# Seeding of old sums, staging rows, operand splits and the first group's order in a fused attention + MLP kernel

## The chip, the cores and the metric

The kernel runs on one core of a Trainium2 chip. The metric is the time of one execution in microseconds of device time. The kernel before took a median of 1314.25 us over three runs (1311.72 to 1316.65).

A core has TensorE (PE: matmuls from SBUF into PSUM), VectorE (DVE), ScalarE (ACT), GpSimd (POOL) and SyncE (SP). Each works through its own queue in program order and waits on semaphores. DMAs are issued from the queues of SP and POOL; those that add to their destination ("accumulating" DMAs) are issued from POOL.

## What is computed

x is 2048 x 576, float32. The reference, cut to what matters:

```python
def A(x):                                   # wqkv 576 x 1728, wo 576 x 576
    q, k, v = heads(x @ wqkv)               # 32 heads of 18
    logits = q . k[s - 2*w], w = 0..7       # sliding window of 8, dilation 2
    return softmax(logits) @ v -> @ wo

def B(x):                                   # w1, w2 576 x 576, w3 576 x 4608, w4 4608 x 576
    x1 = x + shift4(gelu(layernorm(x) @ w1)) @ w2
    return x1 + gelu(layernorm(x1) @ w3) @ w4

xn = layernorm(x)
out = x + A(xn) + B(xn)
```

## The kernel before, in words

**Number format.** Operands of matmuls are split into a rounded high part and a low part, and a product is the sum of high·high, high·low and low·high. With 576 = 4.5 blocks of 128 rows this makes 14 matmuls for one contraction (PAIRS), 7 for one over half the channels (HALVES). A "split" is: ScalarE writes the high part, VectorE subtracts it from the raw value.

**Stages.** (1) QKV, 0 to 195 us: for each token block of 128, `q_cg` and `q_half` make column groups of 432 and 864 of x @ wqkv; `q_half` uses the two banks of a PSUM tile, 512 and 352 columns. (2) Mixing by w1 and w2, 195 to 313 us. (3) Phase 1 of the big MLP, 313 to 535 us: 16 windows u = 0 .. 15 (z = u - 16). A window makes two "up" tiles (`up`: 14 matmuls of 512 columns, then GELU by ScalarE to a high part and a full copy, and VectorE's low part) and four "down" tiles of the window before (`down`: 12 matmuls of 288 columns for a token block of 128, in both banks of a PSUM tile). (4) Phase 2, 535 to 1241 us: 28 groups q = 0 .. 27 of seven products (`product`, 7 matmuls each), named P1, P2, P6, P5, P7, P4, P3, in the manner of Strassen: sums of quarters of xn (A: B11, B21, B22, T1 to T4) against sums of weight blocks (`combine` makes them from w3 in place in the tile w3st; `split_a` and `split_s` split them to w3a and w3s). Results are added over products in Z1 to Z4 (`keep` copies by ScalarE, `z_add` adds by VectorE), then GELU (`gelu12`, `gelu22`: high part; `low12`, `low22`: low part), and eight down tiles D0 to D7 of the group before, in between the products. A group takes some 24 us. The first group has the four down tiles of the last window instead. (5) Output projection by wo, 1241 to 1312 us. The attention itself runs on VectorE in small steps behind the phases (`bg`), paced by a debt to which `spent` is charged.

**Where the sums live.** The 16 row blocks of the result are summed over windows and groups. For ten of them (YD = 1, 2, 3, 5, 7, 9, 10, 11, 13, 15) the sum is in DRAM (yd): ScalarE drains PSUM into a staging row (L870) and POOL issues an accumulating DMA from it to yd[t] (L871). In phase 1 from window 2 on and in phase 2 the staging rows are three rows of the tile Y, 9, 11 and 10 (`EV[0]`), used in turn: a drain waits until the DMA of three drains before has read its row. For the other six (t = 0, 4, 6, 8, 12, 14) the sum is in SBUF, in Y[:, t]: before the tile's matmuls ScalarE copies the old sum into PSUM ("seed", `ahead`, L846), the matmuls add to it, and ScalarE copies the whole back (L873).

**Order.** `ahead` makes the PSUM tile that is needed next as soon as a down tile has been drained: three tiles are in turn in phase 1, two in phase 2. So the seed of the tile after next, or the first matmul of an unseeded one, waits for the drain of the tile that had the bank. Everything is issued in program order, and where a split of an operand stands in the code it stands in ScalarE's queue. In phase 1 `get_op` loads the first operands B11, B21, T3, T2, T1 by SP, and `split_op` splits them in the last two windows. In phase 2 `plan` hangs such steps behind the items of a group's order string (`ORDER`, `ORDERS`).

**Other queues.** `load_xa(t)` adds x into yd[t] by an accumulating DMA of POOL (L880), once for each t of YD, in windows 4 to 13. `sums` makes the operand sums T1 to T4 in DRAM, by DMAs of SP and POOL (L900, L901). In each split of weights POOL issues a small accumulating DMA from w3st into w3a or w3s (L963), and `combine` (L955) can overwrite w3st only after it.

Of the kernel before, what the change touches and what calls it, by code (L numbers as in the profile page):

```python
# [57 lines left out]
def fused_block(ctx, tc, x, wqkv, wo, w1, w2, w3, w4, out):  # L58
# [259 lines left out]

    def q_half(t, h):
        ps = psb.tile([128, 2, 512], F32, name="ps", tag="b")  # L320
        xs, c = lhs(t), 2 * h * CG
        for i, (a, b) in enumerate(PAIRS):
            for k, (n0, n1) in enumerate(((0, 512), (512, 2 * CG))):
                pe.matmul(ps[:, k, :n1 - n0], xs(a), WQ[:, b, c + n0:c + n1],  # L324
                          start=i == 0, stop=i == len(PAIRS) - 1)
        stg = qpool.tile([128, 2 * CG], F32, name="stg", bufs=4)
        act.copy(stg, ps.rearrange("p i c -> p (i c)")[:, :2 * CG])  # L327
        if t == NT - 1 and h == 1:
            get(("z", 1), ring_block(("z", 1)))
        spill(stg, t, 2 * h * CG, 2 * CG)  # L330
# [506 lines left out]
    def halves(t):  # L837
        return Y[:, t, :].rearrange("p (h c) -> p h c", h=2)

    def ahead():  # L840
        n = bank["next"]
        if n < len(bank["order"]):
            t = bank["order"][n]
            ps = bank["make"](n)
            if t not in YD:
                act.copy(ps[:, :, :HF], halves(t))  # L846
            bank["open"].append((t, ps))
            bank["next"] = n + 1

    def begin_downs(order, bufs, make):  # L850
# [4 lines left out]

    def down(t, parts):
        col = slice(t % 4 * 128, (t % 4 + 1) * 128)
        due, ps = bank["open"].pop(0)
        assert due == t
        seq = []  # L860
        for h, w in parts:
            seq += [(h[:, 0], w, 0), (h[:, 0], w, 1), (h[:, 1], w, 0)]
        for n, (h, w, p) in enumerate(seq):
            for k in range(2):
                pe.matmul(ps[:, k, :HF], h[:, col], w[:, p, k * HF:(k + 1) * HF],  # L865
                          start=n == 0 and t in YD, stop=n == len(seq) - 1,
                          skip_group_check=True)
        if t in YD:
            e = staging()
            act.copy(e.rearrange("p (h c) -> p h c", h=2), ps[:, :, :HF])  # L870
            pool.dma_start(yd[t], e, accum_op=ALU.add)  # L871
        else:
            act.copy(halves(t), ps[:, :, :HF])  # L873
        ahead()

    xagain = {}
# [117 lines left out]
    XADD = {5: 0, 6: 4, 7: 8, 8: 12, 10: 6, 12: 14}  # L994
    for u, (c, b) in enumerate(units):
        if u == 1:
            begin_downs([4 * units[v][1] + j for v in range(NU - 1) for j in range(4)], 3,
                        lambda n: psb.tile([128, 2, 512], F32, name="ps", tag="b"))
        if u == 2:
            EV[0] = (9, 11, 10)  # L1000
            ntp.__exit__(None, None, None)
            ap_pool = apc.__enter__()
            state["gen"] = attention(ap_pool)
            next(state["gen"])
        z = u - NU
        if z == -2:
            rtemps[:] = [2, 13, 15]
        r = 0.0 if u < 4 else (RATE[0] if z < -2 else RATE[1]) / 6
        for i in range(C):
            bg(r - spent[0], False)  # L1010
            spent[0] = 0.0
            up(u, c, b, i)
            if u % 4 == 3 and i == 1 and c < NPL - 1:
                split_w3(2 * c + 3)
            if (u, i) == (0, 0):
                get_n(2, x1n[2])
                load_w3p(1, (0,))
            for t in LATE.get((u, i), ()):
                n_turn(t, ntpool)
            if (u, i) == (0, 1):  # L1020
                get_n(3, x1n[3])
            if (u, i) == (3, 0):
                pool.dma_start(yd[13], Y[:, 13, :])
                pool.dma_start(yd[15], Y[:, 15, :])
            if (u, i) in ((1, 0), (2, 1)):
                split_n(u + 1, x1n[u + 1], 0, RT)
            if z == -2:
                split_op(0, ("B11", "B21")[i])
            if z == -1:
                split_op(0, ("T2", "T1")[i])  # L1030
            if (z, i) == (-1, 1):
                x1 = ring_block(("w", 1))
                for sb in range(2):
                    area[sb].update(T4=x1[:, 0:5, :], B22=x1[:, 5:10, :])
                get_op(0, "B22")
                get_op(0, "T4")
        if u == 1:
            raw = x1n[3].bitcast(F32)
            pool.tensor_tensor(RS[2][:, 0, 0:1], raw[:, 4, 0:1], raw[:, 8, 0:1], op=ALU.mult)
        for j, (t, parts) in enumerate(prev):  # L1040
            bg(r - spent[0], j % 2 == 1)
            spent[0] = 0.0
            down(t, parts)
            if (u, j) == (2, 0):
                load_w3p(1, (1,))
                load_w4(1)
            if (u, j) == (3, 1):
                next(state["gen"])
            if u in (1, 2) and j == 1:
                split_n(u + 1, x1n[u + 1], 1, RT)  # L1050
            for f in {(-3, 1): (lambda: split_a(0),), (-3, 2): (lambda: split_w4(NPL),),
                      (-3, 3): (lambda: combine(0),),
                      (-2, 1): (lambda: split_op(0, "T3"),), 
                      (-1, 0): (lambda: split_s(0, (0, 1)),), (-1, 1): (lambda: split_s(0, (2,)),),
                      (-1, 2): (lambda: load_pair(1),)}.get((z, j), ()):
                f()
            if u % 4 == 2 and j == 1 and c < NPL - 1:
                split_w3(2 * c + 2)
# [18 lines left out]
        if z == -2:  # L1077
            x0 = ring_block(("w", 0))
            for sb in range(2):
                area[sb].update(T2=x0[:, 0:5, :], T1=x0[:, 5:10, :])  # L1080
            for k in ("T2", "T1"):
                get_op(0, k)
# [15 lines left out]
    begin_downs([4 * units[NU - 1][1] + j for j in range(4)]  # L1098
                + [8 * (g // NWP) + (j + 4) % 8 for g in range(2 * NWP) for j in range(8)], 2,
                lambda n: qpd.tile([128, 2, 512], F32, name=f"ps{n % 2}"))  # L1100
    Z1, Z2, Z3, Z4 = temp(13), temp(15), temp(5), temp(7)
    NQ = 2 * NWP
# [64 lines left out]
    def o_turn(t):  # L1167
# [275 lines left out]
```

## Time and profile before

| | us |
|---|---|
| median of three runs | 1314.25 |
| the profiled execution | 1313.82 |
| its span, first to last instruction | 1312.0 |
| TensorE busy | 1263.2 |
| VectorE busy | 905.5 |
| ScalarE busy | 766.1 |
| POOL busy | 259.1 |

The profile is of one execution. Busy times of engines overlap, so they don't add up to the span: the engine with the largest share, and what it waits for, tell what sets the time. The mean granted clock of TensorE over the span was 0.988 of full speed. In rows of the timeline the brackets give the idle time of the engine before the row and what ended it.

### The profile page before, as it was taken

What the parts mean: (1) busy time and instruction counts of PE and PEld (TensorE: products, weight loads), DVE (VectorE), ACT (ScalarE), POOL (GpSimd) and SP (SyncE); (2) the same over time, 40 slices, a digit from 0 to 9 for tenths busy, and PEclk for the clock granted to TensorE, in tenths of its full rate; (3) what the DMA queues carried; (4) which work ended last, traced back from release to release, by engine and by line L of the source; (5) the groups of instructions that cost most, each with busy time, mean ns of one, the idle gap of its engine ahead of it and who ended that gap; (6) DMA issues with size and microseconds to landing.
All of it is one profiled execution on the core that took longest, in us unless ns stands there. A gap on an engine that the chain in (4) does not pass through costs nothing.

```text
span 1312.0 us, 20032 instructions
## 1 busy us (share of the span) xinstructions
PE 1263.2 (96%) x7482; PEld 1148.2 (88%) x7482; DVE 905.5 (69%) x1194; ACT 766.1 (58%) x1220; POOL 259.1 (20%) x374
## 2 busy tenths in 40 slices
PE   8999999999999897789999999998999999999998
PEld 8988888899898786688898998987989999989898
DVE  6456535778368795449999999988999974446342
ACT  4322236436645545667677777768768767667730
POOL 2011100021123221112222222212222222222100
PEclk9999999999999898899999999999999999999999
DMA  7646874256788998568978777796776866899982
GB/s 212 153 107 151 171 156 144 71 162 178 175 257 199 197 202 224 103 156 143 223 172 179 185 157 141 174 248 159 149 164 140 172 126 126 200 213 218 254 251 82
DMA packets 204641, 226.14 MB, mean 172 GB/s; under 512 B 79856, under 2 KB 139728, under 8 KB 204416
## 3 DMA queue, kind: packets, MB, share of 16 engines
q1 hardware_dynamic: 171408, 157.60, 41.9%
q0 software_dynamic: 33136, 67.26, 31.8%
q8 instruction: 59, 0.97, 0.3%
q14 instruction: 38, 0.31, 0.1%
HBM read 125.76 MB, written 107.28 MB: 178 GB/s over the span
## 4 chain that ended last, share of the span: by engine, by line
PE 63%; DMA 14%; issue 8%; ACT 6%; DVE 5%; SPq 2%; POOL 2%; POOLq 0%; ACTq 0%; DVEq 0%
PE ps L865 20%; PE cc L1112 12%; PE ps L324 10%; PE p L830 6%; PE ps L214 6%; PE ps L470 4%; DMA w3st<-in_B_w_dram 3%; PE ps L313 3%; DMA w3a<-w3st 3%; DMA x1n<-xn 2%; POOL yd L871 1%; DMA Y<-in_B_w_dram 1%; DMA Y<-od 1%; DMA yd<-Y 1%; DVE w3st L955 1%
## 5 line engine op out<-in xcount | busy, mean ns | idle before, releaser
L865 PEld LDWEIGHTS ps<-w,c 128*128 128x128 f32 x3456 | 482.7, 190 | 50.6 <-ACT Y L870 23.5
L865 PE MATMUL ps<-w,c 128*128 128x288 f32 x3456 | 497.5, 297 | 29.7 <-ACT Y L870 21.4
L871 POOL DMA_DIRECT2D yd<-Y x154 | 138.9, 926 | 413.1 <-ACT Y L870 354.6
L824 DVE TENSOR_TENSOR c<-Y,c 128x512 fp32r<-128x512 f32 x144 | 98.8, 686 | 81.6 <-ACT Y L813 73.5
L1112 PE MATMUL cc<-xt,w3s 128*128 128x512 f32 (+1 forms) x588 | 149.3, 393 | 0.0
L870 ACT COPY Y<-ps 128x576 f32<-128x576 f32 x154 | 97.7, 636 | 74.7 <-PE ps L865 56.9
L324 PE MATMUL ps<-WQ,xt 128*128 128x512 f32 (+1 forms) x672 | 134.9, 360 | 0.0
L324 PEld LDWEIGHTS ps<-WQ,xt 128*128 128x128 f32 x672 | 116.7, 188 | 14.7
L1112 PEld LDWEIGHTS cc<-xt,w3s 128*128 128x128 f32 (+1 forms) x588 | 107.6, 188 | 21.1 <-DVE Y L1122 0.4
L1112 PE MATMUL cc<-x1n,w3a 128*128 128x512 f32 x392 | 100.1, 395 | 2.3 <-ACT cc L1304 2.3
L873 ACT COPY Y<-ps 128x576 f32<-128x576 f32 x108 | 68.9, 638 | 39.8 <-PE ps L865 38.4
L744 DVE TENSOR_TENSOR po<-q,k 128x2304 f32<-128x2304 f32 (+1 forms) x40 | 82.9, 2074 | 8.8 <-DMA k<-qkvd 6.3
L1112 PEld LDWEIGHTS cc<-x1n,w3a 128*128 128x128 f32 x392 | 70.7, 188 | 15.1 <-ACT cc L1304 2.7
L747 DVE TENSOR_REDUCE L<-po 128x128 f32<-128x2304 f32 (+1 forms) x40 | 82.8, 2070 | 0.6
L121 POOL TENSOR_TENSOR rs<-rs,mhalf 128x1 f32<-128x1 f32 x48 | 31.0, 645 | 258.8 <-DVE rs L120 147.8
L327 ACT COPY stg<-ps 128x864 f32<-128x864 f32 x24 | 21.2, 882 | 102.9 <-PE ps L324 60.2
L955 DVE TENSOR_TENSOR w3st<-w3st 128x384 f32<-128x384 f32 x108 | 60.2, 557 | 27.2 <-issue 16.1
L720 DVE TENSOR_TENSOR po<-v,L 128x1152 f32<-128x1152 f32 x56 | 75.4, 1354 | 1.0
L846 ACT COPY ps<-Y 128x576 f32<-128x576 f32 x108 | 69.6, 645 | 2.7
L724 DVE TENSOR_TENSOR po<-po 128x1152 f32<-128x1152 f32 x49 | 66.4, 1355 | 1.0
L1122 DVE TENSOR_TENSOR Y<-cc,Y 128x512 f32<-128x512 f32 x57 | 39.1, 685 | 32.7 <-ACT Y L1118 27.9
L1112 PE MATMUL cc<-x1n,w3s 128*128 128x512 f32 (+1 forms) x196 | 51.6, 404 | 8.7 <-ACT Y L1118 8.7
(193 smaller groups left out, 1889.7 us busy)
## 6 DMA issues: line engine op xcount, KB each, us to landing
yd<-Y POOLq DMA_DIRECT2D x156, 288.0 KB, 6.1
Y<-in_B_w_dram SPq DMA_DIRECT2D x31, 576.0 KB, 6.9
w3st<-in_B_w_dram SPq DMA_DIRECT2D x60, 256.0 KB, 6.4
qkvd<-stg SPq DMA_DIRECT2D x24, 432.0 KB, 3.5
yd<-ev POOLq DMA_DIRECT2D x26, 288.0 KB, 6.5
w3st<-in_B_w_dram SPq DMA_DIRECT2D x108, 64.0 KB, 6.4
xd<-st SPq DMA_DIRECT2D x16, 320.0 KB, 6.1
xd<-big SPq DMA_DIRECT2D x16, 320.0 KB, 8.2
```

The source lines that it names most:

```text
L214: pe.matmul(ps[:, h, :n], xs(a), ws(b, h), start=i == 0, stop=i == len(PAIRS) - 1)
L324: pe.matmul(ps[:, k, :n1 - n0], xs(a), WQ[:, b, c + n0:c + n1], start=i == 0, stop=i == len(PAIRS) - 1)
L720: dve.tensor_tensor(dst, vv, Lf[:, :, w:w + 1].to_broadcast([128, TPP * GH, HD]), op=ALU.mult)
L744: dve.tensor_tensor(dst, qf[:, None, :].to_broadcast([128, n, TPP * GC]), win, op=ALU.mult)
L747: dve.tensor_reduce(Lw[:, w:w + n, :], dst.rearrange("p w (x d) -> p w x d", d=HD), axis=AX.X, op=ALU.add)
L824: dve.tensor_tensor(h[:, 1, :], g, h[:, 0, :].bitcast(F32), op=ALU.subtract)
L830: pe.matmul(ps, W3[f][:, w, :], x1n[b][:, a, :], start=n == 0, stop=n == len(PAIRS) - 1)
L865: pe.matmul(ps[:, k, :HF], h[:, col], w[:, p, k * HF:(k + 1) * HF], start=n == 0 and t in YD, stop=n == len(seq) - 1, skip_group_check=True)
L870: act.copy(e.rearrange("p (h c) -> p h c", h=2), ps[:, :, :HF])
L871: pool.dma_start(yd[t], e, accum_op=ALU.add)
L955: dve.tensor_tensor(st[:, :, o, :], st[:, :, o, :], st[:, :, i, :], op=op)
L1112: pe.matmul(ps, WX[w][:k, v, SLOT[w], :], area[sb][xk][:k, a, :], start=onto is None and i == 0, stop=last and i == len(HALVES) - 1, skip_ ...
```

## The change

Six edits:

1. `q_half` makes its 864 columns as two halves of 432, one in each bank, and ScalarE copies the two halves to the same staging tile.
2. Seeding becomes a choice per tile. A tile that is not in YD is seeded in phase 1 only where its operands come from windows 3 to 11 (`down` runs one window later), and in phase 2 everywhere but for the four tiles of the last window and the tiles that groups 13 and 14 take over from groups 12 and 13 (g + 1 = 13 or 14). That makes 16 unseeded tiles: four with operands of windows 0 to 2, six with operands of windows 12 to 15, six in groups 13 and 14. Where it isn't seeded, the matmuls start at zero and VectorE adds PSUM to Y[:, t] (the new line L873 of the changed kernel).
3. The staging rows are five (9, 11, 10, 13, 15) from window 4 on, and three again from window 13 on (z = -3).
4. `load_xa` of the ten tiles in YD moves from windows 4 to 13 to groups 1 to 10 of phase 2, behind P3.
5. The loads of T2 and T1 are issued within window 14; the splits of the first operands move: B11 and B21 behind the third and fourth down tile of window 14, T3 and T2 behind the up tiles of window 15, T1 behind its fourth down tile.
6. The first group's order ends "D1 D2 P4 D3 P3" instead of "D1 D2 P3 P4 D3", and what hangs behind its items is placed anew.

```diff
 def q_half(t, h):
     ps = psb.tile([128, 2, 512], F32, name="ps", tag="b")
-    xs, c = lhs(t), 2 * h * CG
-    for i, (a, b) in enumerate(PAIRS):
-        for k, (n0, n1) in enumerate(((0, 512), (512, 2 * CG))):
-            pe.matmul(ps[:, k, :n1 - n0], xs(a), WQ[:, b, c + n0:c + n1],
-                      start=i == 0, stop=i == len(PAIRS) - 1)
+    mm_tok(ps, lhs(t), lambda b, i: WQ[:, b, (2 * h + i) * CG:(2 * h + i + 1) * CG], CG)
     stg = qpool.tile([128, 2 * CG], F32, name="stg", bufs=4)
-    act.copy(stg, ps.rearrange("p i c -> p (i c)")[:, :2 * CG])
+    act.copy(stg.rearrange("p (i c) -> p i c", i=2), ps[:, :, :CG])
...
 def ahead():
-    t = bank["order"][n]
+    t, seed = bank["order"][n]
     ps = bank["make"](n)
-    if t not in YD:
+    seed = seed and t not in YD
+    if seed:
         act.copy(ps[:, :, :HF], halves(t))
...
 def down(t, parts):
...
-                      start=n == 0 and t in YD, stop=n == len(seq) - 1,
+                      start=n == 0 and not seed, stop=n == len(seq) - 1,
...
+    elif seed:
+        act.copy(halves(t), ps[:, :, :HF])
     else:
-        act.copy(halves(t), ps[:, :, :HF])
+        spent[0] += 0.75
+        dve.tensor_tensor(halves(t), ps[:, :, :HF], halves(t), op=ALU.add)
     ahead()
...
+    if u == 4:
+        EV[0] = (9, 11, 10, 13, 15)
+    if z == -3:
+        EV[0] = (9, 11, 10)
...
-        if z == -2:
-            split_op(0, ("B11", "B21")[i])
         if z == -1:
-            split_op(0, ("T2", "T1")[i])
+            split_op(0, ("T3", "T2")[i])
+        if (z, i) == (-2, 1):
+            x0 = ring_block(("w", 0))
...
+            for k in ("T2", "T1"):
+                get_op(0, k)
...
-                  (-2, 1): (lambda: split_op(0, "T3"),), 
+                  (-2, 2): (lambda: split_op(0, "B11"),),
+                  (-2, 3): (lambda: split_op(0, "B21"),),
+                  (-1, 3): (lambda: split_op(0, "T1"),),
...
-    if 4 <= u < 4 + len(YD):
-        load_xa(YD[u - 4])
...
-ORDERS = {0: "P1 P2 D0 P6 P5 P7 D1 D2 P3 P4 D3",
+ORDERS = {0: "P1 P2 D0 P6 P5 P7 D1 D2 P4 D3 P3",
...
     if q == 0:
-        at("P1", split_a, n, (0, 1))
-        at("P2", split_op, 0, "B22")
-        at("P6", split_a, n, (2,))
-        at("P5", split_op, 0, "T4")
+        at("P6", split_op, 0, "T4")
         at("D1", gelu22)
+        at("D1", split_op, 0, "B22")
         at("D2", low22)
-        at("D2", combine, n)
-        at("P4", gelu12)
-        at("P4", split_s, n, (0, 1))
-        at("D3", split_s, n, (2,))
-        at("D3", low12)
-        at("D3", load_pair, q + 2)
+        at("D2", split_a, n, (0, 1))
+        at("P4", split_a, n, (2,))
+        at("D3", combine, n)
+        at("P3", gelu12)
+        at("P3", split_s, n, (0, 1))
+        at("P3", low12)
+        at("P3", split_s, n, (2,))
+        at("P3", load_pair, q + 2)
...
     if 0 < q < 5:
         at("D2", sums, 1, q - 1)
+    if 0 < q <= len(YD):
+        at("P3", load_xa, YD[q - 1])
```

From the function `down` on, the changed kernel's lines stand three or four lower or higher than before: L870 is L867 there, L873 the new add (the copy back is L870), L812 is L808, L1118 is L1122, L1122 is L1126.

How the order of instructions moves, at the places where it matters. **ScalarE in windows 14 and 15** (z = -2, -1). L926 to L928 are the high part of one operand's split, three instructions (x1n_4663 holds B11 and B21, in that order, x1n_4664 is T3); L812 and L813 are GELU; L870 and L873 are drains, L846 is a seed. Before:

```order
L812 ACTIVATE c_4693<-p_4678 128x512
L813 ACTIVATE Y<-p_4678 128x512
L926 ACTIVATE x1n_4663<-x1n_4663 128x1024
L927 ACTIVATE Y<-x1n_4663 32x512
L928 ACTIVATE x1n_4663<-x1n_4663 64x512
L812 ACTIVATE c_4717<-p_4702 128x512
L813 ACTIVATE Y<-p_4702 128x512
L926 ACTIVATE x1n_4663<-x1n_4663 128x1024
L927 ACTIVATE Y<-x1n_4663 32x512
L928 ACTIVATE x1n_4663<-x1n_4663 64x512
L873 COPY Y<-ps 128x576
L870 COPY Y<-ps 128x576
```

and after the change (L867 is the drain to a staging row; x1n_4639 holds B11 and B21, x1n_4640 is T3):

```order
L867 COPY Y<-ps 128x576
L926 ACTIVATE x1n_4639<-x1n_4639 128x1024
L927 ACTIVATE Y<-x1n_4639 32x512
L928 ACTIVATE x1n_4639<-x1n_4639 64x512
L867 COPY Y<-ps 128x576
L926 ACTIVATE x1n_4639<-x1n_4639 128x1024
L927 ACTIVATE Y<-x1n_4639 32x512
L928 ACTIVATE x1n_4639<-x1n_4639 64x512
L808 ACTIVATE c_4783<-p_4768 128x512
L809 ACTIVATE Y<-p_4768 128x512
L926 ACTIVATE x1n_4640<-x1n_4640 128x1024
L927 ACTIVATE Y<-x1n_4640 32x512
```

The splits of B11 and B21 stood between GELU and the window's drains; now they stand behind the drains of window 14's third tile and fourth tile, and T3 behind the first GELU of window 15.

**VectorE at the end of the first group** (q = 0). L955 x4 is `combine(1)`; L1122, in the changed kernel L1126, is `z_add`; L824, in the changed kernel L820, is the low part behind a GELU; L966 is VectorE's half of a split of weights. Before:

```order
L1122 TENSOR_TENSOR Y<-cc_4986,Y 128x512
L824 TENSOR_TENSOR c_4994<-Y,c_4994 128x512
L824 TENSOR_TENSOR c_5027<-Y,c_5027 128x512
L955 TENSOR_TENSOR w3st<-w3st 128x3x128 x4
L1122 TENSOR_TENSOR Y<-cc_4986,Y 128x512
L966 TENSOR_TENSOR w3s<-w3st,w3s 128x1024
L824 TENSOR_TENSOR c_5065<-Y,c_5065 128x512
```

and after:

```order
L1126 TENSOR_TENSOR Y<-cc_4953,Y 128x512
L820 TENSOR_TENSOR c_4961<-Y,c_4961 128x512
L595 SCALAR_TENSOR_TENSOR xt<-xt 128x1024
L595 SCALAR_TENSOR_TENSOR xt<-xt,Y 32x512
L873 TENSOR_TENSOR Y<-ps_4939,Y 128x576
L820 TENSOR_TENSOR c_4989<-Y,c_4989 128x512
L966 TENSOR_TENSOR w3a<-w3st,w3a 128x768
L955 TENSOR_TENSOR w3st<-w3st 128x3x128 x4
L1126 TENSOR_TENSOR Y<-cc_4953,Y 128x512
L820 TENSOR_TENSOR c_5052<-Y,c_5052 128x512
L966 TENSOR_TENSOR w3s<-w3st,w3s 128x1024
```

A split of weights (L966 of w3a) now stands directly ahead of the combine, both ahead of the last `z_add`, and there are two operand subtractions (L595, B22) and a new add (L873) before them.

**POOL around `sums`** in phase 1. L880 is `load_xa`, L871 (L868 in the changed kernel) is the DMA from a staging row, L900 and L901 are `sums`. Before:

```order
L871 DMA yd_90<-Y 128x576
L900 DMA td0T_100<-xn_96 288x512
L901 DMA td0T_102<-xn_97 288x512
L880 DMA yd_88<-in_A_x_dram 128x576
L871 DMA yd_91<-Y 128x576
L871 DMA yd_92<-Y 128x576
L871 DMA yd_93<-Y 128x576
L880 DMA yd_89<-in_A_x_dram 128x576
```

and after:

```order
L868 DMA yd_90<-Y 128x576
L900 DMA td0T_100<-xn_96 288x512
L901 DMA td0T_102<-xn_97 288x512
L868 DMA yd_91<-Y 128x576
L868 DMA yd_92<-Y 128x576
L868 DMA yd_93<-Y 128x576
```

The ten L880 have left this part of the queue; they stand in phase 2, one in each of groups 1 to 10, behind the group's second small weight DMA.

More of the change, by code (lines that the diff above doesn't have):

```diff
@@ L842, in ahead @@
         if n < len(bank["order"]):
-            t = bank["order"][n]
+            t, seed = bank["order"][n]
             ps = bank["make"](n)
-            if t not in YD:
+            seed = seed and t not in YD
+            if seed:
                 act.copy(ps[:, :, :HF], halves(t))
-            bank["open"].append((t, ps))
+            bank["open"].append((t, ps, seed))
             bank["next"] = n + 1
@@ L857, in down @@
         col = slice(t % 4 * 128, (t % 4 + 1) * 128)
-        due, ps = bank["open"].pop(0)
+        due, ps, seed = bank["open"].pop(0)
         assert due == t
@@ L996, in fused_block @@
         if u == 1:
-            begin_downs([4 * units[v][1] + j for v in range(NU - 1) for j in range(4)], 3,
+            begin_downs([(4 * units[v][1] + j, 3 <= v < NU - 4) for v in range(NU - 1)
+                         for j in range(4)], 3,
                         lambda n: psb.tile([128, 2, 512], F32, name="ps", tag="b"))
@@ L1026, in fused_block @@
                 split_n(u + 1, x1n[u + 1], 0, RT)
-            if z == -2:
-                split_op(0, ("B11", "B21")[i])
             if z == -1:
-                split_op(0, ("T2", "T1")[i])
+                split_op(0, ("T3", "T2")[i])
+            if (z, i) == (-2, 1):
+                x0 = ring_block(("w", 0))
+                for sb in range(2):
+                    area[sb].update(T2=x0[:, 0:5, :], T1=x0[:, 5:10, :])
+                for k in ("T2", "T1"):
+                    get_op(0, k)
             if (z, i) == (-1, 1):
@@ L1076, in fused_block @@
                 get_op(0, k)
[L1077 to L1082, printed above, removed]
         if 4 <= u < 12 and u % 2 == 0:
             sums(0, (u - 4) // 2)
-        if 4 <= u < 4 + len(YD):
-            load_xa(YD[u - 4])
         if u + 1 in XADD:
@@ L1097, in fused_block @@
     qpd = qpdc.__enter__()
-    begin_downs([4 * units[NU - 1][1] + j for j in range(4)]
-                + [8 * (g // NWP) + (j + 4) % 8 for g in range(2 * NWP) for j in range(8)], 2,
+    begin_downs([(4 * units[NU - 1][1] + j, False) for j in range(4)]
+                + [(8 * (g // NWP) + (j + 4) % 8, g + 1 not in (NWP - 1, NWP))
+                   for g in range(2 * NWP) for j in range(8)], 2,
                 lambda n: qpd.tile([128, 2, 512], F32, name=f"ps{n % 2}"))
```

## The prediction

> **What bounds the kernel now.** I read the page's top and TensorE's table of waits first (us in all, times, longest):
>
> ```profile
> span 1312.0 us, 20032 instructions
> PE 1263.2 (96%) x7482; PEld 1148.2 (88%) x7482; DVE 905.5 (69%) x1194; ACT 766.1 (58%) x1220; POOL 259.1 (20%) x374
> PE ps L865 <- ACT Y L870: 21.4, 9, 8.5
> PE cc L1112 <- ACT Y L1118: 9.4, 3, 8.2
> ```
>
> TensorE is the bound: it works 1263.2 of 1312.0 us. No matmul goes, so only the 48.8 us in which it is not busy can be recovered, and time in which it is busy but slow. These two waits make 30.8 us: a down tile, or a product, waits until ScalarE has emptied the PSUM bank that it needs. TensorE's own timeline says where (start, length, what, and in brackets the idle time before it):
>
> ```profile
> 332.76 4.87 PE L865 MATMUL ps<-w,c 128*128 128x288 f32 x24 [2.65 <-ACT Y L873]
> ...
> 430.79 3.25 PE L865 MATMUL ps<-w,c 128*128 128x288 f32 x12 [5.67 <-ACT Y L870]
> ...
> 497.99 6.55 PE L830 MATMUL p<-xt,w3s 128*128 128x512 f32 x28
> 504.37 4.92 PE L865 MATMUL ps<-w,c 128*128 128x288 f32 x36
> 517.80 3.25 PE L865 MATMUL ps<-w,c 128*128 128x288 f32 x12 [8.51 <-ACT Y L870]
> 520.84 7.86 PE L830 MATMUL p<-xt,w3s 128*128 128x512 f32 x28
> 528.54 6.50 PE L865 MATMUL ps<-w,c 128*128 128x288 f32 x48
> 534.88 3.40 PE L1112 MATMUL cc<-x1n,w3a 128*128 128x512 f32 x14
> 538.12 1.75 PE L865 MATMUL ps<-w,c 128*128 128x288 f32 x12
> ...
> 565.83 1.33 PE L865 MATMUL ps<-w,c 128*128 128x288 f32 x8 [1.07 <-DVE c L824]
> ...
> 588.70 3.25 PE L865 MATMUL ps<-w,c 128*128 128x288 f32 x12 [2.27 <-ACT Y L870]
> ```
>
> Call the stalls S0 (2.65 us), S1 (5.67), S2 (8.51), S3 (the 8.2 of the waits, near 551) and S4 (2.27). Undisturbed, a down tile takes (534.88 - 528.54)/4 = 1.6 us, a product (538.12 - 534.88)/2 = 1.6, a pair of up tiles 504.37 - 497.99 = 6.4. After a stall the 12 matmuls of a down tile take 3.25: TensorE then runs at half rate for some 3 us, so a stall costs its length and about 1.6 more. [...]
>
> **The change, part by part.**
>
> *Balanced columns in QKV* (14 pairs of 512+352 become 432+432). The nearest rows are from the chain of waits; 28 matmuls at L313 are 14 pairs of 432, the 56 at L324 are 28 pairs of the old form:
>
> ```profile
> 52.55 5.42 PE ps L313 x28
> ...
> 63.88 11.04 PE ps L324 x56
> ```
>
> 5.42/14 = 387 ns a pair against 394. L324 issues 672 matmuls, 336 pairs: 336 x 7 ns = 2.4 us, in full, since TensorE sets the pace there; the other end is 0. ScalarE's copy keeps its 864 columns. [...]
>
> *Five staging rows, no x loads in phase 1.* S1 by queue, ScalarE's row and then POOL's:
>
> ```profile
> 430.10 0.64 ACT L870 COPY Y<-ps 128x576 f32<-128x576 f32 x1 [7.47 <-DMA yd<-Y]
> 417.04 0.90 POOL L901 DMA_DIRECT2D td0T<-xn  x1 [5.33 <-issue]
> 417.62 1.15 POOL L880 DMA_DIRECT2D yd<-in_A_x_dram  x1
> 423.71 2.67 POOL L871 DMA_DIRECT2D yd<-Y  x3 [4.93 <-issue]
> ```
>
> ScalarE waits 7.47 us for a staging row whose DMA, three drains earlier, was issued only at 423.71, because POOL's queue stood at L901 and the x load. With five rows the drain needs a DMA five drains back, which is a window earlier (a window drains 2 or 3 rows), and L880 is gone. The stall goes with its half rate: 5.67 + 1.6 = 7.3. The other end is 0, if the two POOL waits named "issue" stay and reach five drains back.
>
> *Unseeded tiles.* 16 of the tiles whose sums live in SBUF lose ScalarE's seed copy and drain copy (32 instructions) and get one VectorE add. A copy of that size took 0.64 above; the add from PSUM that this trace has:
>
> ```profile
> L638 DVE TENSOR_TENSOR Y<-ps,Y x16: 717/750/758, 260.5 to 318.7; 128x576 f32<-128x576 f32 x16
> ```
>
> So 32 x 0.64 = 20 us leave ScalarE and 16 x 0.75 = 12 join VectorE. Neither is the bound on average; the places count. At S0 the window's third tile waits for tile 0's drain, and ScalarE's queue is held by an operand's split. VectorE drains tile 0 now, so the third tile can start; the fourth still needs tile 1's drain copy, which follows the same split, for about 1 us. Gain 1.6 to 3.3; I take 2.5.
>
> *Splits moved, first group reordered.* What is late at S2 and S3: two rows of the chain, then ScalarE's timeline:
>
> ```profile
> 499.03 13.14 DMA x1n<-xn
> ...
> 537.60 8.28 DMA w3st<-in_B_w_dram
> 514.34 1.05 ACT L926 ACTIVATE x1n<-x1n 128x1024 fp32r<-128x1024 f32 x1
> ...
> 516.60 0.62 ACT L873 COPY Y<-ps 128x576 f32<-128x576 f32 x1
> ```
>
> S2: operand B11 lands at 512.2 (499.03 + 13.14), and ScalarE has two splits queued ahead of the drains that the down tile needs. S3: the copy that frees a product's bank stands behind the split of a weight block that lands at 545.9. The change puts both waits behind those drains. But each split still takes ScalarE 516.60 - 514.34 = 2.3 us, and now they stand together: from 512.2 the rest of B11 1.3, a drain 0.5, B21 2.3, two GELUs 1.0, T3 2.3, GELUs 1.0, T2 2.3: 522.9. VectorE ends its half of T2 half a microsecond later, and behind that stands the new add of tile 0 (0.75): 524.1. The window's fourth tile reuses that bank. TensorE would reach it at 522.1: the 36 matmuls end at 509.3, then a tile 1.6, up tiles 6.4, three tiles 4.8. So S2 turns into a **new stall of about 2 us**; that tile ends at 525.7.
>
> Group 0 (seven products, four tiles, 17.7 us) then runs to 543.4. At its end VectorE's order has weight combine(1) ahead of the Z2 addition, from which the next down tile's operand is made. The combine overwrites what POOL's small DMA L963 reads, and waits for it (its median to landing, a long one from the chain, and VectorE's wait for that):
>
> ```profile
> w3a<-w3st POOLq DMA_DIRECT2D x27, 48.0 KB, 4.4
> 574.45 9.51 DMA w3a<-w3st
> 584.04 2.34 DVE L955 TENSOR_TENSOR w3st<-w3st 128x384 f32<-128x384 f32 x4 [5.86 <-DMA w3a<-w3st]
> ```
>
> The DMA, issued about 543.1, lands at 547.5; combine 2.3, Z2 0.7 and GELU 0.7 make it 551.2, its low part 1.2 later. Group 1's first tile could start at 545.0, so a **second new stall of 4 to 6 us**: the tile ends at 553.4, or 555 with half rate, against 567.16 before (565.83 + 1.33). Gain over S2 and S3 together 12 to 14; I take 13.5. The ends: no new stall, tile done at 544.6, 22.5; or the DMA at 9.51, 5 us less, 8.5.
>
> S4 keeps its cause (the 9.51-us DMA), and load_pair(2) is issued some 3 us later in relation to group 1, behind the last split: -3 to 0, I take -1.
>
> *The middle.* In groups 13 and 14 ScalarE has seven splits among the drains (stretch, TensorE, its loads, VectorE, ScalarE, POOL; at the end clock, DMA share, GB/s):
>
> ```profile
> 690.00:880.00 190.00, 188.83 (x1129) 171.26 (x1129) 179.93 (x176) 138.87 (x217) 46.11 (x54) 1.00 0.80 179
> 880.00:920.00 40.00, 33.88 (x198) 28.96 (x198) 32.15 (x35) 34.74 (x55) 8.74 (x11) 1.00 0.74 173
> ```
>
> Of these 40 us TensorE misses 6.1 and ScalarE works 34.7: it is the bound there. Six tiles lose two copies each, 12 x 0.5 = 6 us, about all that TensorE misses. But six adds go to VectorE, 32.15 busy already, behind attention steps. Ends 0 and 6.1; I take 3.5.
>
> *Ten x loads moved to groups 1 to 10.* Each is an accumulating DMA on POOL's queue (its queue's share, and L880's time to landing):
>
> ```profile
> q0 software_dynamic: 33136, 67.26, 31.8%
> DMA to landing us min/median/max: 4.3/6.0/14.6
> ```
>
> 0.318 x 1312/67.26 = 6.2 us of all 16 engines per MB, 1.8 us for 288 KB: 8% of a 24-us group in which DMA is at 0.80. The load waits for the last DMA on its yd tile, the next one on that tile waits for its landing, and behind these stand the other yd adds, which free staging rows (three again), and the small weight DMAs. TensorE misses 1.2 of 190 us there, so there is slack: a row drained at D5 is needed again by the next group's D1, three products and a tile or more later, some 6 us against the 6.0 to landing. Mostly hidden: -3 to 0, I take -1.
>
> **The sum:** 2.4 + 7.3 + 2.5 + 13.5 - 1 + 3.5 - 1 = 27.2 us off the span of 1312.0: 1284.8. That execution took 1313.8 in all, 1.8 outside the span, and lies 0.4 under the median of 1314.25, so I say 1284.8 + 1.8 + 0.4 = **1287 us**.
>
> **Rivals.**
>
> *All stalls go.* VectorE has its adds in time and the combine's DMA lands early; VectorE is only two thirds busy, but the two queue orders above speak against it. 2.4 + 7.3 + 3.3 + 22.5 + 3.9 (S4 with half rate) + 6.1 = 45.5: 1269.
>
> *The waits move rather than go.* The combine's DMA takes 9.5, S4 grows by 3, the middle's adds queue behind attention, QKV gives nothing, the loads cost 3: 7.3 + 2.5 + 8.5 - 3 - 3 = 12.3: 1302.
>
> *Rows were not S1's cause.* The POOL waits of 5.33 and 4.93 us reach five drains back: 1287 + 7.3 = 1294.
>
> *Slower.* The x loads: if each holds POOL's queue beyond that slack, the rows come free too late and tiles stall as at S1 in each group from 1 to 10. At 14.6 us to landing instead of 6.0 some 4 us a group is thinkable: 40 lost against 28.2 gained, 1326. It decides from 2.8 us a group on. Against: phase 1 had the same ten beside a busier queue and shows one such stall.
>
> **How the numbers follow.** Chances: the forecast 0.50 (own range 1279 to 1295), no stall left 0.13, waits moved 0.23, S1 stays 0.06, slower 0.06, something else 0.02. The range 1273 to 1303 holds the first, S1's case, a third of the second and most of the third. A measurement here can tell 0.5% (6.6 us) from no change: faster by more 0.89, within 0.5% 0.05 (the upper tail of moved waits), slower 0.06.
>
> **What would show it.** In the changed profile: no wait of 2 us near 430; the fourth tile of the window after 515 waiting 2 us for VectorE's new add; a wait of 4 to 6 us at group 1's first tile for VectorE's GELU part behind L955; S4 still there; half the idle time in groups 13 and 14; groups 1 to 10 still 24.1 us. Groups longer by tenths (the loads), or new waits in the middle as long as those removed, would prove me wrong.

## The result, and the profile after

The changed kernel took a median of 1315.51 us (1310.43 to 1319.98, 20 runs) against 1316.39 us before (1311.72 to 1318.92, 20 runs): a ratio of 0.9994 with a 95% interval of 0.9982 to 1.0007. No change that can be measured, where the prediction said 1287 us, 1273 to 1303. The page of the changed kernel's profiled execution (1311.86 us, span 1310.0) begins so:

```profile
span 1310.0 us, 20001 instructions
PE 1265.2 (97%) x7482; PEld 1157.0 (88%) x7482; DVE 916.5 (70%) x1210; ACT 747.5 (57%) x1188; POOL 258.6 (20%) x374
```

ScalarE lost 18.6 us of work and VectorE gained 11.0, about as worked out (20 and 12). TensorE's table of waits looks much better than before at first sight:

```profile
PE ps L862 <- ACT Y L867: 12.1, 7, 3.5
PE cc L1116 <- DVE Y L1126: 10.0, 4, 5.7
PE ps L862 <- ACT c L814: 3.2, 1, 3.2
PE ps L862 <- ACT ps L843: 3.2, 6, 1.4
PE cc L1116 <- ACT cc L1310: 2.6, 2, 2.3
```

The wait for the staging drain (L867 now, L870 before) fell from 21.4 to 12.1 us and the 9.4 us of products behind L1118 are gone from the top. A new one has come, 10.0 us of products that wait for VectorE's `z_add` (L1126). TensorE's timeline of the changed kernel shows where:

```profile
514.51 3.39 PE L1116 MATMUL cc<-x1n,w3a 128*128 128x512 f32 x14
...
539.87 3.68 PE L862 MATMUL ps<-w,c 128*128 128x288 f32 x12 [3.22 <-ACT c L814]
...
565.30 1.85 PE L862 MATMUL ps<-w,c 128*128 128x288 f32 x12 [2.04 <-ACT Y L867]
566.99 1.78 PE L1116 MATMUL cc<-x1n,w3a 128*128 128x512 f32 x7
...
600.69 1.89 PE L1116 MATMUL cc<-x1n,w3a 128*128 128x512 f32 x7 [2.25 <-ACT cc L1310]
...
718.24 3.36 PE L1116 MATMUL cc<-xt,w3s 128*128 128x512 f32 x7 [5.67 <-DVE Y L1126]
...
794.92 1.88 PE L1116 MATMUL cc<-xt,w3s 128*128 128x512 f32 x7 [2.08 <-DVE Y L1126]
...
877.12 8.95 PE L862 MATMUL ps<-w,c 128*128 128x288 f32 x48 [3.46 <-ACT Y L867]
```

Group 0 begins at 514.51 where it began at 534.88 before, and group 2 at 566.99 where it began at 591.74: 24.75 us earlier. The old trace ran through groups 3 to 12 nearly without a stop; the changed one does not. The same matmuls can be counted off in both traces (49 product matmuls a group). The lead is how much earlier a group's first product starts than the same product before:

| group | 0 | 1 | 2 | 3 | 7 | 8 | 11 | 13 | 14 | 15 | 18 | 19 | 27 |
|---|---|---|---|---|---|---|---|---|---|---|---|---|---|
| lead, us | 20.4 | 29.4 | 24.8 | 20.8 | 21.3 | 13.7 | 10.9 | 9.7 | 6.6 | 4.8 | 2.6 | 1.5 | 2.0 |

So the gain was made, all of it, by 567 us, and then nearly all given back: 4.0 in group 2, 7.6 in group 7, 2.3 and 1.2 in groups 10 and 11, 4.9 in groups 13 and 14, 3.3 in 17 and 18. The table of stretches of the changed kernel says the same for the whole:

```profile
415.00:435.00 20.00, 20.00 (x121) 18.24 (x120) 18.06 (x13) 9.35 (x16) 4.41 (x5) 1.00 1.06 199
...
690.00:880.00 190.00, 175.02 (x1028) 158.10 (x1027) 166.43 (x165) 126.89 (x197) 45.16 (x53) 0.96 0.80 180
880.00:920.00 40.00, 37.18 (x204) 32.73 (x204) 29.87 (x31) 28.65 (x46) 8.52 (x10) 0.93 0.60 118
```

From 415 to 435 TensorE works all 20 us (14.3 before); from 690 to 880 it works 175.0 of 190, with 1028 matmuls where there were 188.8 and 1129.

What holds `z_add` up in group 7 is read from VectorE's timeline of the changed kernel:

```profile
708.50 2.56 DVE L740 TENSOR_TENSOR po<-q,k 128x2304 f32<-128x2304 f32 x1 [6.98 <-DMA od<-po]
711.10 2.56 DVE L743 TENSOR_REDUCE L<-po 128x128 f32<-128x2304 f32 x1
713.57 0.68 DVE L820 TENSOR_TENSOR c<-Y,c 128x512 fp32r<-128x512 f32 x1
714.16 0.95 DVE L966 TENSOR_TENSOR w3a<-w3st,w3a 128x768 fp32r<-128x768 f32 x1
715.03 2.55 DVE L740 TENSOR_TENSOR po<-q,k 128x2304 f32<-128x2304 f32 x1
717.50 0.68 DVE L1126 TENSOR_TENSOR Y<-cc,Y 128x512 f32<-128x512 f32 x1
```

An attention step (L740) stands in VectorE's queue and waits 6.98 us until the DMA that writes the last batch of heads to DRAM (od<-po) has read the buffer that it overwrites. Everything of the group on VectorE stands behind it. SyncE's queue of the changed kernel, and the chain of waits, show why that DMA is late:

```profile
694.77 1.49 SPq L944 DMA_DIRECT2D w3st<-in_B_w_dram  x2
696.31 2.51 SPq L947 DMA_DIRECT2D w3st<-in_B_w_dram  x4
698.86 0.57 SPq L722 DMA_DIRECT2D od<-po  x1
```

```profile
698.86 9.55 DMA od<-po
```

It is issued directly behind the six DMAs of a weight load (`load_pair`, 4 us of issuing, 768 KB) and takes 9.55 us to land: 698.86 + 9.55 = 708.41, and L740 starts at 708.50. In the old trace the same DMA stood elsewhere in its group:

```profile
692.68 1.01 SPq L944 DMA_DIRECT2D w3st<-in_B_w_dram  x2
693.73 3.27 SPq L947 DMA_DIRECT2D w3st<-in_B_w_dram  x4
697.11 0.55 SPq L564 DMA_DIRECT2D Y<-in_B_w_dram  x1
702.98 0.57 SPq L726 DMA_DIRECT2D od<-po  x1
```

There it follows that load by 6 us and stands ahead of the next one. The median time to landing of the seven such DMAs (the last number of each row) is, before, after the change and in the run e9 below:

```profile
od<-po SPq DMA_DIRECT2D x7, 576.0 KB, 6.1
od<-po SPq DMA_DIRECT2D x7, 576.0 KB, 9.2
od<-po SPq DMA_DIRECT2D x7, 576.0 KB, 6.5
```

VectorE's table of waits has, before,

```profile
DVE po L744 <- DMA od<-po: 2.0, 1, 2.0
```

and after the change

```profile
DVE po L740 <- DMA od<-po: 16.8, 4, 7.0
```

No edit touches the attention. Its place in the program is set by `bg`: at every item it is given a budget less `spent`, and the changed `down` adds 0.75 to `spent` for each new add. Ten adds stand in windows 1 to 15 and group 0, and the nine of them after the attention has begun charge it 6.75 us. Another edit takes a part of that away: the split of T1, which charges 1.9, now stands behind phase 1's last call of `bg`, and the line `spent[0] = 0.0` ahead of phase 2 wipes its charge. So by the account the attention is 6.75 - 1.9 = 4.85 us of work later from group 1 on; the traces have 3.9 to 5.4 us less attention work done at the `z_add`s of groups 2 to 12. The six adds of groups 13 and 14 charge 4.5 more. Its batch now ends behind, not ahead of, a group's weight load: in SyncE's order before

```
L726 DMA od<-po 2048x1x72
L697 DMA v<-qkvd 128x1152
L700 DMA v<-qkvd 128x1008
L944 DMA w3st<-in_B_w_dram 128x2x256 x2
L947 DMA w3st<-in_B_w_dram 32x2x256 x4
```

and after

```
L944 DMA w3st<-in_B_w_dram 128x2x256 x2
L947 DMA w3st<-in_B_w_dram 32x2x256 x4
L722 DMA od<-po 2048x1x72
L693 DMA v<-qkvd 128x1152
L696 DMA v<-qkvd 128x1008
```

### The profile page after: what moved, and what is told of

It is laid out like the page before. It is cut to its first block, busy times and chain, and to the rows that moved or that the text cites. A ratio compares the mean times of both kernels' runs of the same rounds, so it can differ in the third digit from the quotient of the medians.

```text
span 1310.0 us, 20001 instructions
## 1 busy us (share of the span) xinstructions
PE 1265.2 (97%) x7482; PEld 1157.0 (88%) x7482; DVE 916.5 (70%) x1210; ACT 747.5 (57%) x1188; POOL 258.6 (20%) x374
## 4 chain that ended last, share of the span: by engine, by line
PE 44%; issue 11%; DMA 6%; DVE 5%; ACT 3%; POOL 3%; SPq 0%; POOLq 0%; DVEq 0%; ACTq 0%
PE ps L862 20%; PE cc L1116 13%; PE p L826 6%; PE ps L214 4%; DMA w3a<-w3st 3%; POOL yd L868 2%; DVE w3st L955 1%; DMA w3st<-in_B_w_dram 1%; DMA od<-po 1%; ACT Y L867 1%; DMA x1n<-xd 1%; DMA yd<-Y 1%; DVE po L740 1%; DVE w L570 0%; DVE po L716 0%
## 5 line engine op out<-in xcount | busy, mean ns | idle before, releaser
L862 PEld LDWEIGHTS ps<-w,c 128*128 128x128 f32 x3456 | 482.4, 190 | 42.3 <-ACT Y L867 14.5
L862 PE MATMUL ps<-w,c 128*128 128x288 f32 x3456 | 496.5, 297 | 21.3 <-ACT Y L867 12.1
L868 POOL DMA_DIRECT2D yd<-Y x154 | 141.3, 933 | 422.1 <-ACT Y L867 366.4
L1116 PE MATMUL cc<-xt,w3s 128*128 128x512 f32 (+1 forms) x588 | 152.2, 399 | 10.0 <-DVE Y L1126 10.0
L820 DVE TENSOR_TENSOR c<-Y,c 128x512 fp32r<-128x512 f32 x144 | 98.9, 687 | 78.2 <-ACT Y L809 68.9
L867 ACT COPY Y<-ps 128x576 f32<-128x576 f32 x154 | 97.7, 635 | 71.6 <-PE ps L862 59.8
L214 PE MATMUL ps<-WQ,xt 128*128 128x432 f32 x672 | 134.8, 360 | 0.0
L214 PEld LDWEIGHTS ps<-WQ,xt 128*128 128x128 f32 x672 | 125.6, 188 | 5.7
L740 DVE TENSOR_TENSOR po<-q,k 128x2304 f32<-128x2304 f32 (+1 forms) x40 | 83.0, 2075 | 17.4 <-DMA od<-po 16.8
L955 DVE TENSOR_TENSOR w3st<-w3st 128x384 f32<-128x384 f32 x108 | 60.2, 557 | 30.0 <-issue 13.3
L870 ACT COPY Y<-ps 128x576 f32<-128x576 f32 x92 | 58.8, 639 | 33.0 <-PE ps L862 31.6
L843 ACT COPY ps<-Y 128x576 f32<-128x576 f32 x92 | 59.3, 645 | 3.9 <-DVE Y L873 1.5
L1126 DVE TENSOR_TENSOR Y<-cc,Y 128x512 f32<-128x512 f32 x57 | 39.1, 685 | 28.0 <-ACT Y L1122 26.7
L214 PE MATMUL ps<-W,h 128*128 128x288 f32 x384 | 53.5, 295 | 0.0
```

Of the source, the lines that this page charges most:

```text
L214: pe.matmul(ps[:, h, :n], xs(a), ws(b, h), start=i == 0, stop=i == len(PAIRS) - 1)
L740: dve.tensor_tensor(dst, qf[:, None, :].to_broadcast([128, n, TPP * GC]), win, op=ALU.mult)
L820: dve.tensor_tensor(h[:, 1, :], g, h[:, 0, :].bitcast(F32), op=ALU.subtract)
L955: dve.tensor_tensor(st[:, :, o, :], st[:, :, o, :], st[:, :, i, :], op=op)
L1116: pe.matmul(ps, WX[w][:k, v, SLOT[w], :], area[sb][xk][:k, a, :], start=onto is None and i == 0, stop=last and i == len(HALVES) - 1, skip_ ...
```

## The experiments

Three theories: A, the shift of the attention gave the gain back; B, the x loads on POOL's queue in groups 1 to 10 did; C, VectorE has no room for the new adds. Ratios are to the kernel before, in the same session, with the 95% interval; the changed kernel's is 0.9994.

**The attention put back by pace (e1).**

```diff
-    RATE = [12.4, 0.0]
+    RATE = [13.2, 0.0]
```

> The changed kernel with the attention's pace in phase 1 raised from 12.4 to 13.2 us of work per window, which in program order puts back the 6.75 us by which the new adds' charges held the attention back by the first group: each batch's output DMA (od<-po) stands ahead of the weight loads of its group again. Theory A (the attention's place): VectorE's 16.8 us of waits for od<-po fall under 4 us, the stalls of 5.7, 2.1, 1.9 and 1.9 us near 718, 795, 906 and 987 go with their half rate, and the time falls by 10 to 14 us, to 1302-1306. Theory B (the x loads on POOL's queue in groups 1 to 10): the attention's place doesn't matter, within 3 us of 1315.5. Theory C (VectorE has no room for the adds): within 3 us of 1315.5 too.

1298.27 us, 0.9864 (0.9838 to 0.9890): 17 us gained by one number, more than expected. The pace holds in ten windows (u = 4 to 13), so it gives 8.0 us: the attention is not only put back but stands some 3 us ahead of its old place. The stalls near 718 and 795 are gone; but VectorE still waits for od<-po, now in one long and one short wait:

```profile
DVE po L740 <- DMA od<-po: 9.3, 2, 7.1
```

The long one falls in group 3, where the lead drops from 21.5 to 13.4 us. Theory A's sign and size hold, its account of the waits only in part.

**The kernel before with the attention held back (e2).**

```diff
-    RATE = [12.4, 0.0]
+    RATE = [11.65, 0.0]
```

> The kernel before with the attention's pace in phase 1 lowered from 12.4 to 11.65, which holds the attention back by the same 6.75 us in program order and changes nothing else. Theory A: the same waits for od<-po appear in it, near groups 7, 10 and 17, and it is 8 to 14 us slower than before, 1324-1330. Theories B and C: no change, within 4 us of 1316.4.

1322.48 us, 1.0046 (1.0032 to 1.0061): slower, as A alone says, though by 6 us and not 8 to 14. VectorE's table of waits in it:

```profile
DVE po L744 <- DMA od<-po: 21.5, 5, 6.0
```

From 2.0 to 21.5 us without any other edit. The shift is 0.75 us in each of ten windows, 7.5 us, and so larger than the change's own 4.85. The smaller loss is explained by a gain that I had not foreseen: with less attention in phase 1 it reaches group 2 13.6 us earlier than before, and then loses 23.6 us to the start of group 27.

**No x loads at all (e3).** The ten calls of `load_xa` behind P3 are taken out, which leaves x out of ten row blocks of the output.

```diff
-        if 0 < q <= len(YD):
-            at("P3", load_xa, YD[q - 1])
```

> The changed kernel without the ten accumulating DMAs that add x into yd (the output lacks x in ten of sixteen row blocks). Theory A: only the two stalls of group 2 shrink, 2 to 5 us faster, 1311-1314, and the od<-po waits stay over 12 us. Theory B: most of what was lost after group 1 comes back, 15 to 22 us faster, 1294-1301.

1309.75 us, 0.9944 (0.9924 to 0.9964): 6 us, not 20, so B is no explanation of the whole. Group 2 loses 0.3 us of lead instead of 4.0, group 7 still loses 7.4, and 15.1 us of waits for od<-po stay. By the medians the loads cost 6 us altogether; the prediction had 1, at most 3.

**A longer cover for the output DMA (e4).** The attention's third step takes two taps at once and needs the half of its buffer that od<-po reads. Two steps of one tap use the other half.

```diff
-                for w, n in ((0, 1), (1, 1), (2, 2), (4, 2), (6, 2)):
+                for w, n in ((0, 1), (1, 1), (2, 1), (3, 1), (4, 2), (6, 2)):
```

> The changed kernel with the attention's third step (two taps at once, which needs the half of its buffer that the output DMA still reads) cut into two steps of one tap each, which use the other half: the first instruction that must wait for od<-po comes 5.4 us of VectorE's work later, for 0.3 us more work a batch. Theory A: the waits for od<-po fall by 5 us each to under 4 us in all, 8 to 13 us faster, 1303-1308. Theories B and C: not faster, within 3 us.

1303.38 us, 0.9902 (0.9887 to 0.9916): 12 us gained. VectorE's table of waits has no od<-po any more, and group 7 loses 1.4 us of lead instead of 7.6. ScalarE's and POOL's instructions stand in the same order as in the changed kernel. On SyncE a few DMAs stand elsewhere, and on VectorE the two more, smaller steps a batch shift other instructions against the attention in several places. So the run is strong evidence that the wait for od<-po costs most of the 12 us, but not all of them are shown to be that wait.

**Both (e5).**

> The changed kernel with both edits of e1 and e4: the attention ahead again, and the longer cover. Theory A: e1's remaining wait for od<-po (9.3 us, in group 3) goes, so it ends 4 to 8 us below e1's 1298.3, at 1290-1294. If instead the attention's place had worked in another way than through od<-po, it stays within 2 us of e1 (1296-1300).

1291.64 us, 0.9810 (0.9786 to 0.9834). It lies 6.6 us under e1, within the 4 to 8 that A expected. Its lead is 25.7 us at group 2 and 25.8 at group 27: on balance nothing is given back any more. Against e4 the attention's place is worth another 12 us, beyond od<-po. Of the 14.5 us by which the leads of the two differ at group 27, groups 2 and 3 make 5.7 and groups 13 and 14 make 5.6.

In groups 2 and 3 e4's lead falls from 24.2 to 18.1 us and e5's from 25.7 to 25.3. Both wait at the same product, e4 (first row) 1.2 us longer; and only in e4 the seven matmuls then take twice their time:

```profile
601.17 3.36 PE L1116 MATMUL cc<-x1n,w3a 128*128 128x512 f32 x7 [3.89 <-ACT cc L1310]
...
596.41 1.88 PE L1116 MATMUL cc<-x1n,w3a 128*128 128x512 f32 x7 [2.71 <-ACT cc L1310]
```

From group 13 to 15 e4's lead falls from 14.8 to 12.1 and e5's grows from 22.4 to 25.3. In e4's timeline of TensorE the new adds are what the down tiles wait for there, twice:

```profile
866.30 6.42 PE L862 MATMUL ps<-w,c 128*128 128x288 f32 x36 [2.34 <-DVE Y L873]
...
885.33 2.33 PE L862 MATMUL ps<-w,c 128*128 128x288 f32 x12 [3.75 <-DVE Y L873]
```

and in e5's once for long, with shorter waits for ScalarE after it:

```profile
859.74 9.73 PE L862 MATMUL ps<-w,c 128*128 128x288 f32 x60 [3.45 <-DVE Y L873]
869.88 1.85 PE L862 MATMUL ps<-w,c 128*128 128x288 f32 x12 [0.41 <-ACT Y L867]
```

Which attention steps stand ahead of an add would explain that; no run isolates it.

**The x loads back in phase 1 (e6).** e4 with

```diff
-        if 0 < q <= len(YD):
-            at("P3", load_xa, YD[q - 1])
...
+        if 4 <= u < 4 + len(YD):
+            load_xa(YD[u - 4])
```

> e4 with the ten x loads put back into windows 4 to 13, the five staging rows kept. If the loads in groups 1 to 10 cost what the traces suggest (stalls of 3.9 us and more in group 2 and after, some 6 us in all) and five rows alone cure the stall near 430: 4 to 8 us faster than e4's 1303.4, 1295-1299. If the loads were also part of the stall near 430: it returns with 5 to 7 us and the time is 1301-1306.

1301.65 us, 0.9901 (0.9865 to 0.9937), the same as e4. No stall returns near 430, so the five rows alone cure it. But the expected gain does not come: e6 reaches group 2 4.7 us later than e4 and is level with it from group 4 on. Moving the loads out of phase 1 gained about what it cost later.

**Groups 13 and 14 seeded again (e7).** e4 with

```diff
-                + [(8 * (g // NWP) + (j + 4) % 8, g + 1 not in (NWP - 1, NWP))
+                + [(8 * (g // NWP) + (j + 4) % 8, True)
```

> e4 with the six tiles of groups 13 and 14 seeded by ScalarE and drained by it again, as before the change. Theory that the unseeding helps in the middle: ScalarE's queue delays the drains again and it is 2 to 4 us slower than e4, 1305-1307. Theory that VectorE's adds stall there (waits on L873 of 2.3 and 3.8 us in e4): 1 to 5 us faster, 1298-1302.

1303.78 us, 0.9911 (0.9884 to 0.9937), not told apart from e4. The run changes two things at once: the six adds go, and with them 4.5 us of charges, so from group 13 on the attention also stands elsewhere than in e4. What the unseeding alone is worth is read from e10.

**The combine behind Z2 (e8).** e4 with the first group's plan as

```diff
-            at("D3", combine, n)
             at("P3", gelu12)
-            at("P3", split_s, n, (0, 1))
             at("P3", low12)
+            at("P3", combine, n)
+            at("P3", split_s, n, (0, 1))
             at("P3", split_s, n, (2,))
```

> e4 with the first group's combine placed behind the Z2 addition, its GELU and its low part on VectorE. The wait of 3.2 us at group 1's first down tile goes with its half rate, 1.9 us: 3 to 5 us faster than e4, 1298-1300, unless the weights that the combine makes are then late for group 1, which would leave a wait of the products on w3s and no gain (1302-1305).

1302.42 us, 0.9901 (0.9879 to 0.9922). Its profiled execution reaches group 2 3.1 us earlier than e4's and the 3.2-us wait for L814 is gone from its top waits; a wait of 2.86 us for ScalarE's copy (L1310) at the next product takes a part of its place. The medians can't be told apart: a gain of 0 to 3 us.

**Only the charge taken out (e9).** Every instruction of the changed kernel stays; only the accounting line goes.

```diff
         else:
-            spent[0] += 0.75
             dve.tensor_tensor(halves(t), ps[:, :, :HF], halves(t), op=ALU.add)
```

> The changed kernel without the line that charges each new add 0.75 us to the attention's budget; every instruction stays, only the attention's place in the program order goes back to that of before. Theory A (the charge shifted the attention): as e1, 12 to 18 us faster than the changed kernel, 1297-1303. If e1's gain came from the higher pace itself and not from the place: no change, 1313-1317.

1296.38 us, 0.9844 (0.9826 to 0.9862): 19 us faster than the changed kernel, by a line that issues nothing. It waits 5.4 us in all for od<-po. Since T1's charge stays wiped, its attention stands 1.9 us ahead of its place before the change, not exactly in it. This is the direct test of the cause: the charge alone costs some 19 us.

**All tiles seeded again (e10).** The changed kernel with True for all three conditions on seeding: no adds, no charge, the attention as in e9.

> The changed kernel with every such tile seeded by ScalarE again, in all sixteen places, so that no add is left and nothing is charged; the attention stands as in e9. Theory A: the attention's place is worth most of the loss, so it is also faster than the changed kernel, 1299-1305, and it differs from e9 by the unseeding alone: 2 to 6 us slower than e9, by the stall near 333 and by groups 13 and 14. If it equals e9 within 2 us, the unseeding itself is worth nothing.

1301.61 us, 0.9886 (0.9866 to 0.9905). Against e9, which has the attention in the same place, the unseeding itself is worth 5.2 us, 3.4 of them in groups 13 and 14 (from group 13 to 15 e9's lead grows by 4.0, from 12.4 to 16.4, and e10's by 0.6, from 10.8 to 11.4). It does pay, once its side effect is out.

**The best found (e11, e12).** e5 with e8's plan, and the same with a pace of 14.0.

> e5 with e8's order of the first group: attention ahead, longer cover, combine behind the Z2 addition. If e8's 3 us in its trace hold without the attention's waits: 2 to 4 us faster than e5, 1287-1290. If the weights are then late in group 1 or 2 or the attention's place is disturbed: equal to e5 or slower, 1291-1296.

> e11 with the attention's pace in phase 1 at 14.0 instead of 13.2, another 7 us of work ahead by the first group. If being ahead is good as such: 2 to 5 us faster than e11. If only the place of the output DMA to the weight loads counts (there it stands ahead of them still, but earlier in the group): within 2 us of e11; if phase 1 or the middle lose by it, 2 to 8 us slower.

e11: 1288.76 us, 0.9793 (0.9771 to 0.9814), the fastest of all, 2.1% under the kernel before; from e5 it can't be told apart. Its page begins

```profile
span 1285.6 us, 20017 instructions
PE 1256.7 (98%) x7482; PEld 1151.4 (90%) x7482; DVE 917.8 (71%) x1226; ACT 748.4 (58%) x1188; POOL 259.0 (20%) x374
```

e12: 1294.77 us, 0.9827 (0.9805 to 0.9849), 6 us slower than e11 by the medians. Its timeline has one long wait more, in group 3, where it loses 6.5 us of lead and e11 none:

```profile
601.04 3.35 PE L1116 MATMUL cc<-x1n,w3a 128*128 128x512 f32 x7 [6.62 <-ACT cc L1310]
```

That copy stands in ScalarE's queue behind a drain to a staging row, whose DMA POOL issued late (ScalarE's row, then POOL's):

```profile
599.86 0.64 ACT L867 COPY Y<-ps 128x576 f32<-128x576 f32 x1 [7.35 <-DMA yd<-Y]
591.65 0.91 POOL L901 DMA_DIRECT2D td1T<-xn  x1 [11.66 <-issue]
```

POOL's queue stood 11.66 us at the operand sums there; in e1, with the pace of 13.2, it stood 6.53. Why longer is not shown. Being further ahead is not good as such.

## Why the prediction was wrong

Up to the start of group 2 its sum was right, and its terms can be checked one by one by the lead of matching matmuls in the two traces:

| term | predicted | measured |
|---|---|---|
| QKV columns | 2.4 | 0.1 |
| S0, unseeded tile 0 | 2.5 | 1.8 |
| S1, five rows | 7.3 | 7.5 |
| S2, S3 and S4 to the start of group 2 | 13.5 - 1 | 15.4 |
| sum at group 2 | 24.7 | 24.8 |
| the middle, groups 13 and 14 | +3.5 | -4.9 (+4.0 in e9) |
| x loads | -1 | -6 (e3) |
| the attention's place | not in the sum | -19 (e9, with the middle's part) |

The last three rows overlap and can't be added. That 24.7 and 24.8 agree is in part luck: the QKV term was 2.3 too high and the term below it for S2 to S4 2.9 too low. The middle's term was right where the attention is not pushed back: e9 against e10 has 3.4 us for it.

**The step that failed** is that of the unseeded tiles: "32 x 0.64 = 20 us leave ScalarE and 16 x 0.75 = 12 join VectorE. Neither is the bound on average; the places count." I looked at the places of the adds and not at the place of what the adds push away. The line `spent[0] += 0.75` was in the diff. The attention is one long program whose steps are dealt out by that account; 6.75 us of charges, 4.85 net, moved all of it against the groups, and its output DMA past the weight loads in SyncE's queue. VectorE then waited 16.8 us for that DMA instead of 2.0. e9 undoes the charge alone and has 19 us back; e2 makes a larger shift of the same kind in the old kernel and gets such waits too. With the charge out, e9's 1296.38 us is 9 us above the forecast, and its lead at group 27 is 16.1 us. The sentence "groups 1 to 10 still 24.1 us" of the last part rested on the same omission, and the rivals had no case for it: the slower one named groups 1 to 10, where 13.9 of the 22.8 us were lost, but put all on POOL's queue.

**The x loads** were rightly named as a cost and mis-sized. "Mostly hidden: -3 to 0, I take -1": e3 has 6 us, of which 3.7 fall in group 2. There the changed kernel's POOL queue stands 5.25 us at L901 (the operand sums of the second half, which are in that place before too) and then 4.43 at the load:

```profile
591.17 0.91 POOL L901 DMA_DIRECT2D td1T<-xn  x1 [5.25 <-issue]
...
598.31 0.85 POOL L880 DMA_DIRECT2D yd<-in_A_x_dram  x1 [4.43 <-issue]
```

Each group's slack was reckoned alone and not with the sums.

**The QKV term** was read from another loop, 28 matmuls of `q_cg`. In the place that was changed the pace is the same within 1 ns a pair (the last 70 pairs take 27.83 us before and 27.81 after), and mixing starts at

```profile
195.02 9.72 PE L470 MATMUL ps<-xt,W 128*128 128x512 f32 x42
```

before, and after the change at

```profile
194.88 9.71 PE L466 MATMUL ps<-xt,W 128*128 128x512 f32 x42
```

0.14 us earlier over 336 pairs. The term's other end, 0, was the nearer one.

**The new stalls** were foreseen: the fourth tile near 512 waits 0.2 us for VectorE's add where I had 2, and group 1's first tile 3.2 for the GELU behind the combine where I had 4 to 6.

**The rivals.** "Rows were not S1's cause" is out: e6 has the loads back and no such stall. "The waits move rather than go" had the right kind of end and the wrong mechanism; its 1302 was still 13 us too fast.

**What stays open:** the 12 us between e4 and e5. Where they are lost is seen, mostly in groups 2, 3, 13 and 14, but the two differ in the place of all attention steps from window 4 on, and no run takes apart which of these steps does it. Why POOL's queue stands longer at the operand sums in some runs is open too.

## What to carry to other kernels

Where background work is dealt out by an account of time, every line that charges the account moves that work. Here charges of 0.75 us, 12 us over the whole kernel, cost 19. Compare the order of all queues, DMA queues too, before and after, also in the stretches that the diff doesn't touch. Where a buffer is read by an outgoing DMA and overwritten by the next batch, look for waits of the engine that overwrites it: here VectorE waited 16.8 us in four of them, 6.98 in one, with everything behind it in its queue, and e4, whose first steps of a batch use the other half, was 12 us faster. And check a forecast at several places of the timeline: here the gain was there at 567 of 1310 us and was lost behind it, which the total alone doesn't show.

## What the runs showed of the hardware

The attention's output DMA (576 KB) landed in 5.8 to 10.4 us in the old trace, at a median of 6.1, and at a median of 9.2 in the changed kernel; directly behind six weight DMAs of 768 KB in all it took 9.55.

POOL's queue stood at some accumulating DMAs for a reason that the profile doesn't name: 4.43 us at an x load and 5.25 at an operand sum in the changed kernel, 11.66 at the same sum in e12. At the other nine x loads of the changed kernel it didn't stand. In each of the three places the later DMAs of that queue stood behind the one that was held up.

The half rate after a stall does not come after every one, and no threshold comes out of these rows. In the changed kernel the matmuls after idle times of 2.04 us (12 of them), 2.08 and 2.25 us (7 each) took 1.85 to 1.89 us, about the full rate (1.75 and 1.79 undisturbed); after 3.22 (12) and 5.67 us (7) they took 3.68 and 3.36. But after 2.27 us in the old trace 12 took 3.25, the half rate, and after 2.34 us in e4 36 matmuls took 6.42 us where undisturbed ones take 4.92; after 2.71 us in e5 seven took 1.88, about the full rate. No run here shows what decides it.
